# An attention-and-mixer kernel on one core: the second pair's k by SyncE's queue, U and V rounded later, and the first batch's mixing with two channel blocks side by side

## The chip, the cores and the metric

One core of one Trainium2 chip runs the whole program. The time is the device time of one execution in microseconds; the median over several runs counts. Smaller is better.

## The reference, cut to what matters

```python
# q, k, v: (B, H, S, D) = (8, 8, 576, 64);  beacon_k, beacon_v: (8, 8, 16, 64)
k_all = concatenate([beacon_k, k], axis=2)           # 592 keys
v_all = concatenate([beacon_v, v], axis=2)
scores = q @ k_all.T / sqrt(D)                       # causal over the 576, beacons always seen
x = softmax(scores) @ v_all                          # -> (8, 576, 512), heads side by side
h = (x.transpose(0, 2, 1) @ U @ V).transpose(0, 2, 1)   # U: (576, 32), V: (32, 576): mixes tokens
u = x + h
out = u + maximum(u @ w_ch1, 0) @ w_ch2              # w_ch1: (512, 2048), w_ch2: (2048, 512)
```

## The kernel before, in words

Heads are worked in pairs: `p` counts 32 of them, four to a batch, and pair `p` of a batch has the two heads of "set" `c`, which together fill 128 partitions. For a pair, q and k are turned on TensorE (`qkT_units`), the transposed scores are formed and exponentiated on ScalarE (`score_units`, `visit`), and `av_unit` weights v by them and divides by the sums, into `xb`, the batch's attention output with tokens on partitions in five blocks. A batch's four pairs done, the mixing adds `h` and leaves `u` transposed in `uT` (channels on partitions, in four blocks of 128, all 4608 tokens in the free dimension). The MLP then runs over nine blocks of 512 tokens (`mlp_units`: `gps`, L536, and `cps`, L562).

Everything is issued in an order written out by hand. Each engine works through its own queue in that order; only waits on other engines and on transfers hold it up. The change lies in the first 26 us, where the first batch is worked through while loads come in.

**Loads.** Float32 inputs come in two ways. `load_first` has SyncE's and ScalarE's queues bring set 0 of q and k as float32 into `stq` and `stk` (L205); `regroup` (L270) rounds them to float16 into `pr`. `build_masks` has SyncE bring set 1 of q the same way; a memset of one element of the target by VectorE (L126) holds this load back until VectorE gets there. All other loads of q, k, v and the weights are issued by GpSimd (L205, L220, L191), which rounds them on the way into `st`, `vs` and `w`; these are one after the other in GpSimd's queue, each costing GpSimd the time to issue it. Where a pair's k came through GpSimd, `by_heads` turns it in twelve 64-column matmuls (L283), and where it came through `regroup`, `in_pair` turns it in six (L277).

**U and V.** `small_loads` has SyncE load U in three pieces and V as float32 into one tile, `small` (L169 to L174), behind a memset of one element by VectorE (L167). `cast`, further on, has GpSimd round them into `Usb` and `Vsb` (L178, L179) and SyncE copy `Vsb`'s 32 rows to the three other row blocks of 32 partitions (L183), and V's last 80 columns to four places of `Vend` (L184). `Vend[:, cc, :]` is zero except in row block `cc`. So a matmul over all four row blocks, with `Vend[:, cc, :]` as the moving side, picks out channel block `cc`. In the order, `cast` stands on GpSimd right behind the first quarter of `w_ch1` (`emit_w1(0)`, L191) and ahead of the loads of k and q of batch 1.

**The first batch's mixing.** `first_mix` does it in two halves of two channel blocks each:

- `head(c0, n)`: five matmuls `qtp` (L491), one for each block of tokens, with U as the stationary side (32 columns) and 256 channels of `xb` moving; VectorE rounds the result, 32 x 256, into `qts`, named `qfirst` (L494).
- `begin`: matmuls with the identity turn `xb` into PSUM, 496 tokens into `ups` and the last 80 into `uend` (L415).
- `rest`: for each channel block one matmul adds `h` to `ups` and one to `uend`, from `Vsb`'s first 32 rows (L508); ScalarE or VectorE copies them to `uT`.

The first half stands between the two weightings of pair 2 and those of pair 3, the second behind pair 3's, with the first MLP products (`part`, the first token block's `gps`) in between. The later batches (`mix_units`) work with all four channel blocks at once, in four column blocks and then four row blocks (L436, L461) and with `Vend` (L474).

Of the kernel before, what the change touches and what calls it, by code (L numbers as in the profile page):

```python
# [11 lines left out]
F32 = mybir.dt.float32  # L12
# [6 lines left out]
P = 128  # L19
# [11 lines left out]
def kernel(  # L31
# [13 lines left out]
    nc = tc.nc  # L45
    B, H, S, D = q.shape
    Nb = beacon_k.shape[2]
    DM = H * D
    R = moe_U.shape[1]
# [12 lines left out]
    nq = [min(S, P * (j + 1) - Nb) - q0[j] for j in range(NC)]  # L62
    NT = NC
    QM, NL = q0[NT - 1], nq[NT - 1]
    TJ = 6
    TP = S // TJ
    TB = TP + Nb
# [27 lines left out]
    gtp = ctx.enter_context(tc.tile_pool(name="gtp", bufs=2))  # L95
# [9 lines left out]
    def pst(shape, dtype, name):  # L105

        b = emptied.pop(0)
        t = psum.tile(shape, dtype, tag=f"bank{b}", name=name)
        bank_of[id(t)] = (b, t)
        return t  # L110

    def emptying(t):
        emptied.append(bank_of.pop(id(t))[0])
# [8 lines left out]
    def build_masks():  # L122
        make_identity(nc, ident)
        nc.vector.memset(bigmask[:, 0, P - Nb : P], F16_MAX)
        nc.vector.tensor_copy(out=identb, in_=ident)
        nc.vector.memset(first[1][0:1, 2, 0:1], 0.0)  # L126
        token_load(nc.sync, q[0], first[1], SETS[1])
        make_upper_triangular(nc, mask, val=F16_MAX, diag=True)
        token_load(nc.gpsimd, k[0], Ls[0][0][0], SETS[1])
        nc.vector.tensor_copy(out=bigmask[:, 0, 0 : P - Nb], in_=mask[:, Nb:P])  # L130
        nc.vector.tensor_copy(out=bigmask[:, 1, :], in_=mask)
        for i in range(2):
            nc.vector.tensor_scalar(
                out=negmask[:, i, :], in0=bigmask[:, i, :], scalar1=1.0, scalar2=NEG,
                op0=ALU.is_lt, op1=ALU.mult,
            )
        prs[0] = [None, regroup(first, 0, 1, V, act_copy)]
# [10 lines left out]
    Usb = const.tile([P, NT, R], F16, name="Usb", tag="Usb")  # L148

    Vsb = const.tile([P, S], F16, name="Vsb", tag="Vsb")  # L150
    Vend = const.tile([P, NCC, nq[NT - 1]], F16, name="Vend", tag="Vend")
# [12 lines left out]
    def small_loads():  # L164

        f = utp.tile([P, NT * R + S], F32, name="small", tag="ut")
        nc.vector.memset(f[0:1, 0:1], 0.0)  # L167
        uf, vf = f[:, 0 : NT * R].rearrange("p (j r) -> p j r", r=R), f[0:R, NT * R :]
        nc.sync.dma_start(out=uf[: nq[0], 0, :], in_=moe_U[0 : nq[0], :])  # L169
        nc.sync.dma_start(  # L170
            out=uf[:, 1 : NT - 1, :], in_=moe_U[q0[1] : QM, :].rearrange("(j p) r -> p j r", p=P)
        )
        nc.sync.dma_start(out=uf[:NL, NT - 1, :], in_=moe_U[QM:S, :])
        nc.sync.dma_start(out=vf, in_=moe_V)  # L174

        def cast():
            for rr, jj in ((nq[0], slice(0, 1)), (P, slice(1, NT - 1)), (NL, slice(NT - 1, NT))):
                nc.gpsimd.tensor_copy(out=Usb[:rr, jj, :], in_=uf[:rr, jj, :])  # L178
            nc.gpsimd.tensor_copy(out=Vsb[0:R, :], in_=vf)  # L179
            for cc in range(NCC):  # L180
                rs = ds(R * cc, R)
                if cc:
                    nc.sync.dma_start(out=Vsb[rs, :], in_=Vsb[0:R, :])  # L183
                nc.sync.dma_start(out=Vend[rs, cc, :], in_=Vsb[0:R, QM:S])  # L184

        return cast
# [14 lines left out]
    def beacon_load(eng, src, dst, hs):  # L201
        eng.dma_start(out=dst[0:Nb], in_=src[hs].rearrange("h p d -> p h d"))  # L202

    def token_load(eng, src, dst, hs):
        eng.dma_start(out=dst[0:TP, hs, :], in_=src[hs].rearrange("h (p j) d -> p h (j d)", j=TJ))  # L205

    def key_beacons(eng, src, dst, hs):
        beacon_load(eng, src, dst[TP:TB, hs, (TJ - 1) * D : TJ * D], hs)
# [19 lines left out]
    def by_token(t):  # L228
        return t.rearrange("p h (j d) -> p j h d", j=TJ)
# [3 lines left out]
    def qk_tiles():  # L233

        t = [stage.tile([P, TJ * DM], F16, name=f"st{i}", tag=f"st{i}") for i in range(2)]
        st = [x[:, :].rearrange("p (h e) -> p h e", h=H) for x in t]
        whole = [x[:, 0 : NT * DM].rearrange("p (j h d) -> p j h d", h=H, d=D) for x in t]
        return st, whole
# [24 lines left out]
    def regroup(st, c, i, *copies, beacons=True):  # L263

        t = pairs.tile([P, TJ, 2, D], F16, name=f"pr{i}", tag=f"pr{i}")
        src = by_token(st[i][:, 2 * c : 2 * c + 2, :])
        w = TJ // len(copies)
        for a, copy in enumerate(copies):
            js = slice(w * a, w * (a + 1))
            copy(out=t[0:TP, js], in_=src[0:TP, js])  # L270
        if i == 0 and beacons:
            copies[0](out=t[TP:TB, TJ - 1], in_=src[TP:TB, TJ - 1])
        return t
# [139 lines left out]
    def x_into(xb, ups, cc, js, a, first):  # L413
        for j in js:
            nc.tensor.matmul(  # L415
                ups[:, ds(q0[j] - a, nq[j])], xb[: nq[j], j, ts(cc, P)], ident[: nq[j], : nq[j]],
                start=first and j == js[0], stop=False, skip_group_check=True,
            )
# [64 lines left out]
    def first_mix(xb):  # L483

        qts = outp.tile([P, DM], F16, name="qfirst", tag="ob")
        cell = {}

        def head(c0, n):
            qtp = pst([R, P * n], F32, name="qtp")
            for j in range(NT):  # L490
                nc.tensor.matmul(  # L491
                    qtp, Usb[: nq[j], j, :], xb[: nq[j], j, ds(P * c0, P * n)], start=(j == 0), stop=(j == NT - 1)
                )
            nc.vector.tensor_copy(out=qts[0:R, ds(P * c0, P * n)], in_=qtp)  # L494
            emptying(qtp)

        def begin(c0, cs, n=2):
            for cc in cs:
                cell[cc] = pst([P, QM], F32, name="ups")
                x_into(xb, cell[cc], cc, list(range(NT - 1)), 0, True)  # L500
                if cc == c0:
                    cell["end"] = pst([P, n, NL], F32, name="uend")
                x_into(xb, cell["end"][:, cc - c0, :], cc, [NT - 1], QM, cc == c0)

        def rest(c0, n, copies, end):
            for at in (0, QM):
                for i in range(n):
                    nc.tensor.matmul(  # L508
                        cell["end"][:, i, :] if at else cell[c0 + i], qts[0:R, ts(c0 + i, P)],
                        Vsb[0:R, at : S if at else QM], start=False, stop=True, skip_group_check=True,  # L510
                    )
            for cc, copy in zip(range(c0, c0 + n), copies):
                copy(out=uT[:, cc, 0:QM], in_=cell[cc])
                emptying(cell[cc])
            end(out=uT[:, ds(c0, n), QM:S], in_=cell["end"])
            emptying(cell["end"])

        return head, begin, rest
# [114 lines left out]
    Ls, qTs, xbs = {}, {}, {}  # L633
# [35 lines left out]
    SETS = [slice(2 * c, 2 * c + 2) for c in range(NH2)]  # L669

    first = []

    def load_first():

        kf = gtp.tile([P, 2, TJ * D], F32, name="stk", tag="gT")
        qf = gtp.tile([P, 4, TJ * D], F32, name="stq", tag="gT")
        first.extend([kf, qf])
        for src, dst in ((q[0], qf), (k[0], kf)):
            for eng, h in ((nc.sync, 0), (nc.scalar, 1)):
                token_load(eng, src, dst, slice(h, h + 1))  # L680
        Ls[0] = qk_tiles()
        key_beacons(nc.gpsimd, beacon_k[0], Ls[0][0][0], ALLH)
        nc.scalar.activation(out=warm, in_=ones, func=AF.Exp)
# [4 lines left out]
    prs = {}  # L688
    V = nc.vector.tensor_copy
# [122 lines left out]
    with tc.manual_schedule(engines={ENG.PE, ENG.Activation, ENG.DVE, ENG.SP, ENG.Pool}):  # L812
# [12 lines left out]
        idle(IDLE[4], ident)  # L825
        t0[1]()
        sc[0](IDLE[1], gs=[1, 0])
        prs[1] = [None, regroup(first, 1, 1, V)]
        for u in qkT_of(1):
            u()  # L830
        clear()
        cast = small_loads()
        sc[1]([3, 2], False)
        sc = scores_of(1)
# [1 line left out]

        v_tokens(v[0], vss[0], HALVES[1])
        emit_w1(0)
        cast()
        Ls[1] = qk_tiles()  # L840
        (kt, qt), _ = Ls[1]
        token_load(nc.gpsimd, k[1], kt, HALVES[0])
        token_load(nc.gpsimd, q[1], qt, HALVES[0])
        key_beacons(nc.gpsimd, beacon_k[1], kt, ALLH)
        emit_w1(1)
        token_load(nc.gpsimd, k[1], kt, HALVES[1])
# [26 lines left out]
        head, begin, rest = first_mix(xbs[0])  # L873
# [9 lines left out]
        rest(0, 2, (act_copy, act_copy), act_copy)  # L883
        av = av_of(3)
        av[0]()
        av[1]()
        begin(2, (2,))
        part(D0, 2)
        part(D1, 2)
        head(2, 2)  # L890
# [180 lines left out]
    with tc.If(n_bad != 0, label="general"):  # L1071
        with tc.For_i(0, B, 1) as bi:
            L = qk_tiles()
            qT = qkt.tile([P, NH2, S], F16, name="qT", tag="qT")
            xb = xbp.tile([P, NT, DM], F16, name="xb", tag="xb")
# [11 lines left out]
            for t0 in range(0, S, 512):  # L1087
                n = min(512, S - t0)
# [32 lines left out]
```

## Time and profile before

| | us |
|---|---|
| Median of 3 runs (lowest to highest) | 350.36 (350.11 to 350.96) |
| The profiled execution | 349.7 |
| Its span | 348.0 |
| TensorE busy | 341.3 (98%) |
| VectorE busy | 189.7 (55%) |
| ScalarE busy | 163.6 (47%) |
| GpSimd busy | 97.8 (28%) |

The span is what the profiler sees of the program; the execution's time has 1.7 us around it. Engines are called PE (TensorE's matmuls), PEld (its weight loads), DVE (VectorE), ACT (ScalarE), POOL (GpSimd) and SP (SyncE); a `q` behind a name is that engine's issue of transfers. `L491` is line 491 of the kernel before. In the changed kernel the same statement stands a few lines further down. In the timeline a row is start, length, engine, line, operation, out<-in and count, and in brackets the idle time before it with what ended it. `out<-in` are the names in the program, and `x5` is a group of five instructions, merged.

### The profile page before, as it was taken

The page shows a single profiled execution, that of the slowest core. Times are in us where ns is not written, and L with a number is a line of the kernel's source. Part 1 is how long each engine was busy: PE and PEld are TensorE (multiplying, and loading weights), DVE is VectorE, ACT ScalarE, POOL GpSimd, SP SyncE. Part 2 cuts the span into 40 slices and gives each one's busy share as a digit, 9 for nine tenths or more (in the row PEclk, how much of TensorE's full clock was granted, in tenths as well). Part 3 has the DMA queues.
Part 4 walks back from the last instruction along what each step waited for, and adds up shares of the span by engine and source line. Part 5 has one row for each costly group of instructions (what it writes and reads, how often), then busy time and mean ns, then how long its engine had stood idle before and what let it go on. Part 6 is the DMA issues. An engine that isn't in the chain of part 4 may idle for free.

```text
span 348.0 us, 7791 instructions
## 1 busy us (share of the span) xinstructions
PE 341.3 (98%) x3084; PEld 173.2 (50%) x3084; DVE 189.7 (55%) x493; ACT 163.6 (47%) x358; POOL 97.8 (28%) x137
## 2 busy tenths in 40 slices
PE   8899999999999999999999999999999999999995
PEld 4565565455554455444554445455445444444443
DVE  6676965788875553554465556535655542323311
ACT  6957851578723664167615752494434203202300
POOL 8966714544506457303930130000000000000000
PEclk9999999999999999999999999999999999999999
DMA  9999999999999999991999697713122314013011
GB/s 166 135 186 170 169 200 171 216 148 154 128 142 145 167 133 132 154 213 14 146 139 237 64 117 123 184 38 68 62 75 47 69 62 121 2 60 106 17 66 64
DMA packets 146635, 41.88 MB, mean 120 GB/s; under 512 B 131488, under 2 KB 142080, under 8 KB 146592
## 3 DMA queue, kind: packets, MB, share of 16 engines
q0 software_dynamic: 87440, 18.18, 68.2%
q1 hardware_dynamic: 58928, 22.84, 36.0%
q8 instruction: 26, 0.43, 0.5%
q10 hardware_dynamic: 224, 0.30, 0.2%
q14 instruction: 17, 0.14, 0.1%
HBM read 37.37 MB, written 9.44 MB: 134 GB/s over the span
## 4 chain that ended last, share of the span: by engine, by line
PE 93%; POOL 2%; DMA 2%; issue 1%; DVE 1%; ACT 1%; POOLq 0%
PE gps L536 36%; PE cps L562 35%; PE po L399 8%; PE sps L384 6%; DMA st<-in_q_dram 2%; PE tps L277 1%; PE sps L350 1%; POOL vs L220 1%; PE cph L588 1%; PE qtp L436 1%; POOL st L205 1%; PE tps L283 1%; PE ups L461 1%; PE ups L415 1%; ACT expt L356 0%
## 5 line engine op out<-in xcount | busy, mean ns | idle before, releaser
L536 PE MATMUL gps<-uT,w 128*128 128x512 f16 x576 | 136.0, 379 | 0.1
L562 PE MATMUL cps<-w,gT 128*128 128x512 f16 x560 | 130.9, 379 | 0.0
L390 ACT ACTIVATE expt<-sps 128x496 f16<-128x496 f32 x192 | 82.5, 534 | 71.5 <-PE sps L384 71.5
L549 ACT ACTIVATE gT<-gps 128x512 f16<-128x512 f32 x86 | 50.9, 622 | 78.8 <-PE gps L536 78.6
L536 PEld LDWEIGHTS <-w 128*128 128x128 f16 x576 | 51.8, 98 | 58.0 <-issue 2.4
L562 PEld LDWEIGHTS <-gT 128*128 128x128 f16 x560 | 50.8, 98 | 58.9 <-issue 6.2
L551 DVE TENSOR_SCALAR gT<-gps 128x512 f16<-128x512 f32 x58 | 40.0, 690 | 41.9 <-PE gps L536 40.5
L575 DVE TENSOR_TENSOR ob<-cps,ut 128x512 f32<-128x512 f32 x31 | 21.4, 691 | 48.3 <-PE cps L562 47.5
L220 POOL DMA_DIRECT2D vs<-in_v_dram x50 | 39.6, 810 | 17.1 <-PE gps L536 5.8
L399 PEld LDWEIGHTS <-expt 128*128 128x128 f16 (+1 forms) x960 | 36.2, 98 | 12.7 <-issue 0.8
L399 PE MATMUL po<-vs,expt 128*128 128x65 f16 (+1 forms) x960 | 38.9, 194 | 0.0
L408 DVE TENSOR_TENSOR xb<-po,rec 128x320 f16<-128x320 f32 x64 | 31.5, 492 | 2.2
L326 DVE TENSOR_TENSOR expt<-expt,bigmask 128x512 f16<-128x512 f16 x58 | 24.1, 416 | 6.7 <-ACT expt L390 6.7
L356 ACT ACTIVATE expt<-sps 128x496 f16<-128x496 f32 (+2 forms) x64 | 27.1, 584 | 0.9 <-PE sps L350 0.8
L407 DVE RECIPROCAL rec<-po 128x5 f32<-128x5 f32 x64 | 12.1, 188 | 27.0 <-PE po L399 26.8
L384 PE MATMUL sps<-qT,kT 64*128 64x80 f16 (+4 forms) x288 | 23.3, 281 | 0.1
L202 POOL DMA_DIRECT2D vs<-in_beacon_v_dram x8 | 4.3, 536 | 57.8 <-PE po L399 57.7
L384 PEld LDWEIGHTS <-kT 64*128 64x128 f16 x288 | 9.9, 94 | 18.3 <-issue 14.8
L651 POOL DMA_DIRECT2D st<-in_q_dram x20 | 16.9, 863 | 6.6 <-DMA vs<-in_v_dram 2.7
L651 POOL DMA_DIRECT2D st<-in_k_dram x20 | 17.0, 883 | 3.4 <-DMA st<-in_q_dram 3.4
L448 DVE TENSOR_TENSOR uT<-ups,uT 128x496 f16<-128x496 f32 x24 | 14.5, 667 | 5.0 <-PE ups L461 5.0
L310 DVE COPY qT<-tps 128x576 f16<-128x576 f16 (+1 forms) x16 | 11.8, 736 | 4.6 <-PE tps L283 2.8
(98 smaller groups left out, 161.9 us busy)
## 6 DMA issues: line engine op xcount, KB each, us to landing
out_dram<-ob SPq DMA_DIRECT2D x35, 256.0 KB, 2.3
vs<-in_v_dram POOLq DMA_DIRECT2D x18, 128.0 KB, 6.9
w<-in_moe_w_ch_dram POOLq DMA_DIRECT2D x4, 512.0 KB, 6.1
w<-in_moe_w_ch_dram POOLq DMA_DIRECT2D x2, 1024.0 KB, 13.6
st<-in_k_dram POOLq DMA_DIRECT2D x12, 128.0 KB, 8.6
st<-in_q_dram POOLq DMA_DIRECT2D x12, 128.0 KB, 9.6
st<-in_k_dram POOLq DMA_DIRECT2D x2, 576.0 KB, 13.2
st<-in_q_dram POOLq DMA_DIRECT2D x2, 576.0 KB, 16.1
```

Source lines behind the costliest of these rows:

```text
L220: nc.gpsimd.dma_start(out=dst[a : a + nq[j], j, :, :], in_=src[hs, ds(q0[j], nq[j]), :].rearrange("h p d -> p h d"))
L326: nc.vector.tensor_tensor(out=e4, in0=e4, in1=bigmask, op=ALU.min)
L356: nc.scalar.activation(out=ex[i][:, ds(SLOT * g, gw[g])], in_=ps[g, i][:, 0 : gw[g]], func=AF.Exp, scale=scale)
L384: nc.tensor.matmul(ps[p, g, i][:, ds(o, w)], kT[hp, c, ds(P * ch, P)], qT[hp, c, ds(qa, w)], start=True, stop=True,)
L390: nc.scalar.activation(out=at[p][3][i][:, ds(SLOT * g, gw[g])], in_=ps[p, g, i][:, 0 : gw[g]], func=AF.Exp, scale=scale)
L399: nc.tensor.matmul(po[:, j, :], ex[0 : nk[c], ds(blk[(c, j)], P)], vs[0 : nk[c], ds(c * H * E + h * E, E)], start=(c == 0), stop=(c == j),)
L408: nc.vector.tensor_tensor(out=xb[:, :, ds(h * D, D)], in0=po[:, :, 0:D], in1=r.broadcast_to([P, NT, D]), op=ALU.mult)
L536: nc.tensor.matmul(g[:, 0:n], w1[:, cc, ts(dc, P)], uT[:, cc, ds(t0, n)], start=(cc == 0), stop=(cc == NCC - 1))
L549: nc.scalar.activation(out=gT["t"][:, dc, 0:n], in_=g[:, 0:n], func=AF.Relu)
L551: nc.vector.tensor_scalar_max(out=gT["t"][:, dc, 0:n], in0=g[:, 0:n], scalar1=0.0)
L562: nc.tensor.matmul(ps[:m, :], gT["t"][:, dc, ds(P * i, m)], w2[:, dc, :], start=(dc == 0), stop=turned and dc == NDC - 1, skip_group_check ...
L651: nc.gpsimd.dma_start(out=dst[a : m[j], j, :, :], in_=src[:, ds(q0[j], nq[j]), :].rearrange("h p d -> p h d"))
```

## The change

The set 1 of k (pair 1's) is no longer loaded by GpSimd but by SyncE as float32, behind q's, and rounded on VectorE by `regroup`; its 16 beacon rows are copied by VectorE from where GpSimd loads them. V is loaded twice, into two row blocks of `small`, and GpSimd rounds both at once, so that `Vsb` has two row blocks without a copy. `cast` stands two issues later on GpSimd, behind the loads of k and q of the first half of batch 1's heads. In the first mixing, `head` writes its two channel blocks to two column blocks (64 partitions, 128 columns), and `rest` uses one row block for each channel block, and for the last 80 tokens `Vend` with both row blocks. In the second half `begin(2, (2,))` stands ahead of `av[1]`.

```diff
@@ build_masks
-        nc.vector.memset(first[1][0:1, 2, 0:1], 0.0)
-        token_load(nc.sync, q[0], first[1], SETS[1])
+        for x in first[::-1]:
+            nc.vector.memset(x[0:1, 2, 0:1], 0.0)
+        for x, src in zip(first[::-1], (q[0], k[0])):
+            token_load(nc.sync, src, x, SETS[1])
         make_upper_triangular(nc, mask, val=F16_MAX, diag=True)
-        token_load(nc.gpsimd, k[0], Ls[0][0][0], SETS[1])
@@ small_loads
-        uf, vf = f[:, 0 : NT * R].rearrange("p (j r) -> p j r", r=R), f[0:R, NT * R :]
+        uf, vf = f[:, 0 : NT * R].rearrange("p (j r) -> p j r", r=R), f[0 : 2 * R, NT * R :]
...
-        nc.sync.dma_start(out=vf, in_=moe_V)
+        for i in range(2):
+            nc.sync.dma_start(out=vf[ds(R * i, R), :], in_=moe_V)
 
         def cast():
             for rr, jj in ((nq[0], slice(0, 1)), (P, slice(1, NT - 1)), (NL, slice(NT - 1, NT))):
                 nc.gpsimd.tensor_copy(out=Usb[:rr, jj, :], in_=uf[:rr, jj, :])
-            nc.gpsimd.tensor_copy(out=Vsb[0:R, :], in_=vf)
+            nc.gpsimd.tensor_copy(out=Vsb[0 : 2 * R, :], in_=vf)
             for cc in range(NCC):
                 rs = ds(R * cc, R)
-                if cc:
+                if cc > 1:
                     nc.sync.dma_start(out=Vsb[rs, :], in_=Vsb[0:R, :])
                 nc.sync.dma_start(out=Vend[rs, cc, :], in_=Vsb[0:R, QM:S])
@@ first_mix
         def head(c0, n):
-            qtp = pst([R, P * n], F32, name="qtp")
+            qtp = pst([R * n, P], F32, name="qtp")
             for j in range(NT):
-                nc.tensor.matmul(
-                    qtp, Usb[: nq[j], j, :], xb[: nq[j], j, ds(P * c0, P * n)], start=(j == 0), stop=(j == NT - 1)
-                )
-            nc.vector.tensor_copy(out=qts[0:R, ds(P * c0, P * n)], in_=qtp)
+                for i in range(n):
+                    nc.tensor.matmul(
+                        qtp[ds(R * i, R), :], Usb[: nq[j], j, :], xb[: nq[j], j, ts(c0 + i, P)],
+                        start=(j == 0), stop=(j == NT - 1), skip_group_check=True, tile_position=(0, R * i),
+                    )
+            nc.vector.tensor_copy(out=qts[0 : R * n, ts(c0, P)], in_=qtp)
...
         def rest(c0, n, copies, end):
-            for at in (0, QM):
-                for i in range(n):
-                    nc.tensor.matmul(
-                        cell["end"][:, i, :] if at else cell[c0 + i], qts[0:R, ts(c0 + i, P)],
-                        Vsb[0:R, at : S if at else QM], start=False, stop=True, skip_group_check=True,
-                    )
+            for i in range(n):
+                nc.tensor.matmul(
+                    cell[c0 + i], qts[ds(R * i, R), ts(c0, P)], Vsb[ds(R * i, R), 0:QM],
+                    start=False, stop=True, skip_group_check=True,
+                )
+            for i in range(n):
+                nc.tensor.matmul(
+                    cell["end"][:, i, :], qts[0 : R * n, ts(c0, P)], Vend[0 : R * n, i, :],
+                    start=False, stop=True, skip_group_check=True,
+                )
@@ load_first
-        kf = gtp.tile([P, 2, TJ * D], F32, name="stk", tag="gT")
+        kf = gtp.tile([P, 4, TJ * D], F32, name="stk", tag="gT")
@@ the order
-        prs[1] = [None, regroup(first, 1, 1, V)]
+        prs[1] = [regroup(first, 1, i, V, beacons=False) for i in (1, 0)][::-1]
+        V(out=prs[1][0][TP:TB, TJ - 1], in_=by_token(Ls[0][0][0][:, SETS[1], :])[TP:TB, TJ - 1])
...
         emit_w1(0)
-        cast()
         Ls[1] = qk_tiles()
         (kt, qt), _ = Ls[1]
         token_load(nc.gpsimd, k[1], kt, HALVES[0])
         token_load(nc.gpsimd, q[1], qt, HALVES[0])
+        cast()
         key_beacons(nc.gpsimd, beacon_k[1], kt, ALLH)
...
         av = av_of(3)
         av[0]()
+        begin(2, (2,))
         av[1]()
-        begin(2, (2,))
```

## The prediction

> **What bounds the kernel now.** I read the head of the page first, then the chain that ended last in order of time, then the timeline around the edits, and last the landing times of single transfers.
>
> ```profile
> span 348.0 us, 7791 instructions
> PE 341.3 (98%) x3084; PEld 173.2 (50%) x3084; DVE 189.7 (55%) x493; ACT 163.6 (47%) x358; POOL 97.8 (28%) x137
> 9.22 0.60 POOL st L205
> 9.82 5.47 DMA st<-in_q_dram
> 15.34 0.47 PE tps L283 x12
> 16.64 0.58 PE sps L350 x4
> 18.75 0.65 PE qtp L491 x5
> 20.49 0.52 PE ups L508 x2
> 21.01 0.07 PE uend L508 x2
> 23.23 0.65 PE qtp L491 x5
> 24.68 0.52 PE ups L508 x2
> 16.64:20.85 4.21, 4.21 (x75) 2.97 (x75) 3.90 (x15) 3.59 (x10) 4.21 (x7) 1.00 1.17 173
> 20.85:25.20 4.35, 4.35 (x58) 2.65 (x56) 2.27 (x8) 1.41 (x4) 1.52 (x3) 1.00 1.26 196
> 25.20:36.00 10.80, 10.80 (x151) 5.81 (x149) 7.54 (x15) 8.58 (x20) 7.82 (x11) 1.00 1.60 170
> 48.00:348.00 300.00, 295.91 (x2457) 146.84 (x2453) 155.58 (x382) 126.20 (x273) 63.49 (x80) 1.00 1.01 113
> ```
>
> The first two rows are the page's: TensorE is busy for 341.3 of 348.0 us. The next rows are the chain: start, length, what. Up to 9.82 us it runs through GpSimd's issues, then through one q load that lands at 15.29, and from 16.64 on through TensorE. The last four rows are the busy time of each engine in four stretches (after the stretch and its length: PE, PEld, DVE, ACT, POOL, granted clock, DMA share, GB/s). TensorE has no gap in the first three and 4.1 us of gaps in the last 300. So what the change does to TensorE's queue between 16 and 36 us goes to the end one for one: nothing behind it has room to take a delay up, and work removed there is a gain. Ahead of 16.64 the bounds are loads and ScalarE.
>
> **The second mixing, where the saving counts.** In `head`, five matmuls with 256 moving columns become ten with 128 in two column blocks; in `rest`, the two `ups` matmuls get a row block each. The later batches already work so, with four blocks:
>
> ```profile
> 49.23 0.55 PE qtp L436 x20
> 51.64 0.32 PE ups L461 x4
> 54.80 0.14 PE uend L474 x4
> ```
>
> Twenty narrow `qtp` matmuls take 0.55 us on the chain, so ten take 0.28 where five wide ones took 0.65: 0.37 saved if two blocks run side by side as four do, and nothing if they run one after the other (the same number of columns in all). Four `ups` in four row blocks take 0.32; two in one block took 0.52. Two side by side I put at the length of one, 0.26: 0.26 saved, at most 0.36, at least nothing. The two `uend` matmuls stay at 0.07. I take 0.63 us for each mixing (0 to 0.73). VectorE's copy of `qtp` shrinks too, behind other matmuls, so I count nothing. Moving `begin(2, (2,))` ahead of `av[1]` only reorders work that TensorE does anyway: nothing.
>
> **The first mixing, where a wait is added.** Before, the first `uend` matmuls read `Vsb`, which GpSimd itself writes. Now they read `Vend`, blocks 0 and 1, which two transfers on SyncE's queue copy out of `Vsb` after GpSimd's cast. In before nobody needs `Vend` until 54.80 us (the last row above). Behind the waiting matmul in TensorE's queue stand the two weightings of pair 3, the second mixing and the first MLP products: all the rest of the program. So the question is when those two transfers land. Issue times first:
>
> ```profile
> 9.35 0.06 DVE L167 MEMSET small<- 1x1 f32 x1
> 10.80 0.42 SPq L174 DMA_DIRECT2D small<-in_moe_V_dram  x1
> 14.01 0.82 POOL L191 DMA_DIRECT2D w<-in_moe_w_ch_dram  x1
> 14.74 0.49 POOL L178 CAST Usb<-small 112x32 f16<-112x32 f32 x2
> 15.84 0.66 POOL L179 CAST Vsb<-small 32x576 f16<-32x576 f32 x1
> 16.45 0.68 POOL L205 DMA_DIRECT2D st<-in_k_dram  x1
> 16.52 0.65 SPq L184 DMA_DIRECT2D Vend<-Vsb  x1
> 17.12 0.68 POOL L205 DMA_DIRECT2D st<-in_q_dram  x1
> 17.84 0.59 SPq L184 DMA_DIRECT2D Vend<-Vsb  x1
> 20.85 0.23 PE L508 MATMUL uend<-Vsb,qfirst 32*128 32x80 f16 x2
> ```
>
> GpSimd loses one issue early (some 0.63 us, as the 0.60 at 9.22 shows), and its casts move behind the two 0.68 us issues: by its own queue the casts would start at 14.74 - 0.63 + 1.36 = 15.5. But the cast of V also waits for its load, which in before it started right behind: V issued at 10.80, cast at 15.84. That load is issued after VectorE's memset of `small`, and ahead of this memset VectorE now rounds k of pair 1 (0.55, the same shape as the row at 6.25 below) and its beacons (L272 below: 0.19 to 0.52), and may wait for the load. That is 0.75 to 1.1 us later; the second copy of V adds an issue of 0.42. So the second V is issued at about 12.1, and with before's 5.0 us (below) lands at 17.1; the cast (same columns, 0.66) ends at about 17.8, 17.1 if V lands sooner. The first `Vend` copy is issued then, the second 0.65 later, at about 18.1 (17.7 to 18.5).
>
> Now the landings, each the answer on transfers for the stretch of one issue (the last number: us from issue to landing; for the first three rows, medians over issues in the first 30 us):
>
> ```profile
> Vend<-Vsb SPq DMA_DIRECT2D x4, 5.0 KB, 6.0
> small<-in_moe_V_dram SPq DMA_DIRECT2D x1, 72.0 KB, 5.0
> small<-in_moe_U_dram SPq DMA_DIRECT2D x1, 14.0 KB, 2.3
> Vend<-Vsb SPq DMA_DIRECT2D x1, 5.0 KB, 4.5
> Vsb<-Vsb SPq DMA_DIRECT2D x1, 36.0 KB, 7.7
> Vend<-Vsb SPq DMA_DIRECT2D x1, 5.0 KB, 7.2
> w<-in_moe_w_ch_dram POOLq DMA_DIRECT2D x1, 512.0 KB, 6.2
> st<-in_k_dram POOLq DMA_DIRECT2D x1, 288.0 KB, 5.8
> st<-in_q_dram POOLq DMA_DIRECT2D x1, 288.0 KB, 8.1
> ```
>
> A 5 KB copy took 4.5 us when issued at 16.52 and 7.2 when issued at 17.84: it landed at 21.0, then 25.0. The large loads around it landed at 20.2 (weights, 14.01 + 6.2), 22.3 (k) and 25.2 (q). Landings thus follow the order of issue closely: the first copy came in behind the weights, the next two with the q load issued beside them. In the changed kernel both large k and q issues stand ahead of both copies. So I expect the copies at the time of that q load, 24 to 25; the median of 6.0 gives the same, 18.1 + 6.0 = 24.1, and I take that.
>
> [...]
>
> TensorE would be at `uend` at 20.85 - 0.63 = 20.2. It waits 3.9 us. The first mixing's saving and everything earlier disappears in this wait.
>
> **The front, hidden by that wait.** Pair 1's k now takes 0.55 + 0.19 to 0.52 us more on VectorE, ahead of the copies of qT and kT:
>
> ```profile
> 6.25 0.54 DVE L270 CAST pr<-stq 96x768 f16<-96x768 f32 x1
> 8.81 0.16 DVE L315 COPY kT<-tps 128x16 f16<-128x16 f16 x1
> L272 DVE COPY pr<-st x3: 192/397/520, 35.8 to 59.0; 16x128 f16<-16x128 f16 x3
> 9.19 0.58 PE L350 MATMUL sps<-qT,kT 64*128 64x496 f16 x4
> 10.08 0.67 ACT L356 ACTIVATE expt<-sps 128x496 f16<-128x496 f32 x1
> 17.05 3.39 ACT L356 ACTIVATE expt<-sps 128x496 f16<-128x496 f32 x8 [0.23 <-PE sps L350]
> ```
>
> kT of pair 1 was ready at 8.97; it will be at 9.7 to 10.2. Pair 1's scores started 0.22 after it, at 9.19, and four took 0.58; the first is there some 0.4 to 0.6 us after kT, so at 10.1 to 10.8. ScalarE took it at 10.08: a wait of 0 to 0.7 us, against a gain of at most 0.23 (its idle time at 17.05) from q loads issued 0.63 earlier. Net -0.23 to +0.7 at `uend`, and all of it is covered while the copies land after 21; without that cover it counts.
>
> **The sum.** 24.1 - 20.85 = 3.25 later at `uend`, less 0.63 in the second mixing: +2.6 us. On the profiled execution's 349.7 (span 348.0) that is 352.3. That execution lies 0.66 under the median of the runs, 350.36; on the median it gives **353.0 us**.
>
> **The rivals.**
> - *Landing as the first copy did.* No `Vsb` copy stands ahead of the second `Vend` copy any more, so both may land as the first did: 18.1 + 4.5 = 22.6, or 21.6 with the earlier issue. 22.6 - 20.85 - 0.63 = +1.1: 351.5 (350.5 to 351.5). For it: before's first copy was first on its queue too. Against: it was issued when the large q load was not. 17%.
> - *A longer landing,* 7.2 to 7.7 us, since more is ahead: 18.1 + 7.2 = 25.3 to 25.8, or +3.8 to +4.3: 354.2 to 354.7. 13%.
> [...]
> - *The blocks do not run side by side* (the change doesn't do what it says): no saving in the second mixing, wait as forecast: +3.25, 353.6. Against: the rows at 49.23 and 51.64. 5%.
>
> **How the numbers follow.** The forecast has 55%, with 352.0 to 354.2 for landings of 23.1 to 25.3. No change means within 0.3%, 1.05 us: what a measurement can tell here. Of the first rival, 10 points fall within it and 7 above; the no-wait case is faster; all others are slower. Faster 0.10, same 0.10, slower 0.80. The range 350.5 to 354.6 leaves out the no-wait case and the last end of the long landing.
>
> **What would show it.** Right: a wait of TensorE at the `uend` matmul of the first mixing, released by a `Vend` transfer, of 3 to 5 us, with `Vend` landing at 23 to 25 us; TensorE back to back behind it; ten `qtp` in about 0.3 us and two `ups` in about 0.26. Wrong: `Vend` landing before 21 us, or TensorE's gaps after 36 us shrinking by as much as the wait.

## The result, and the profile after

The changed kernel took 355.28 us (median of 6 runs, 354.83 to 357.31) against 350.66 us of the kernel before, measured beside it: a ratio of 1.0133, 95% interval 1.0101 to 1.0165. It is slower by 4.6 us. Forecast were 353.0 us and at most 354.6, so the direction was right and the size was not. The profiled execution took 354.83 us, its span 353.2 us.

The page's head, its row of granted clock in 40 slices, and the chain that ended last in order of time (start, length, what); one row of before, from the same view, stands apart behind them:

```profile
span 353.2 us, 7803 instructions
PE 342.6 (97%) x3088; PEld 173.7 (49%) x3088; DVE 190.3 (54%) x496; ACT 164.2 (47%) x358; POOL 97.4 (28%) x136
PEclk9899999999999999999999999999999999999999
...
3.32 5.90 DMA stk<-in_k_dram
...
14.02 4.18 DMA small<-in_moe_V_dram
...
18.32 0.67 POOL Vsb L181
19.00 0.65 SPq L186
...
19.70 5.82 DMA Vend<-Vsb
...
25.56 0.19 PE uend L516
...
27.90 0.40 PE qtp L494 x10
...
29.10 0.31 PE ups L511 x2
29.41 0.17 PE uend L516 x2
29.59 0.64 PE tps L285 x24
```

```profile
25.27 0.64 PE tps L283 x24
```

TensorE's busy time is 1.3 us longer than before (342.6 us against 341.3) and the span 5.2 us, so most of the difference is standing still. The chain from 14.0 to 25.5 us no longer runs through TensorE but through the load of V, GpSimd's rounding of it, SyncE's issue, and the landing of the second `Vend` copy at 25.5. From there to the transposes at 29.59 TensorE goes back to back. They begin 4.32 us later than in before, and most of the difference in span, 5.2 us, is there already. Of the remaining 0.9 us, 0.4 are lost by the end of the last matmul (348.7 against 344.0) and 0.5 lie behind it; no run looked for their cause. The wait itself, in the view of who waited for whom, is shorter than forecast:

```profile
PE uend L516 <- DMA Vend<-Vsb: 2.2, 2, 1.7
```

It is 2.2 us, not 3.9, since TensorE reached `uend` only at 23.1, 2.3 us later than before and 2.9 later than I had it. The busy time of TensorE in single microseconds shows where, and how it fared in the wait for `Vend` (after the stretch and its length: busy time, instructions, granted clock, DMA share, GB/s):

```profile
7.00:8.00 1.00, 0.77 (x7) 1.00 1.37 195
8.00:9.00 1.00, 0.32 (x6) 1.00 2.26 157
9.00:10.00 1.00, 0.26 (x7) 1.00 2.04 136
10.00:11.00 1.00, 1.00 (x18) 0.79 0.38 24
11.00:12.00 1.00, 1.00 (x11) 0.50 0.81 64
12.00:13.00 1.00, 1.00 (x7) 0.50 1.21 175
13.00:14.00 1.00, 1.00 (x17) 0.50 1.37 127
...
23.00:24.00 1.00, 0.21 (x2) 1.00 1.19 157
24.00:25.00 1.00, 0.08 (x1) 1.00 1.29 200
25.00:26.00 1.00, 0.56 (x13) 1.00 1.28 222
```

TensorE waited for pair 1's q and k, which landed after 5.1 and 5.9 us, and then the granted clock was 0.50 for 3.4 us. In the wait for `Vend`, and behind it, the clock stayed at 1.00. The late front also made `Vend` late, as VectorE's and SyncE's rows of the timeline show:

```profile
8.07 0.56 DVE L272 CAST pr<-stq 96x768 f16<-96x768 f32 x1 [1.39 <-DMA stq<-in_q_dram]
...
9.24 0.56 DVE L272 CAST pr<-stk 96x768 f16<-96x768 f32 x1 [0.62 <-DMA stk<-in_k_dram]
...
12.08 0.06 DVE L168 MEMSET small<- 1x1 f32 x1
...
13.55 0.89 SPq L176 DMA_DIRECT2D small<-in_moe_V_dram  x2
...
19.00 1.27 SPq L186 DMA_DIRECT2D Vend<-Vsb  x2
```

VectorE waited for q and then for k of pair 1. So its memset of `small` came at 12.08 instead of 9.35, V's second load was issued at 14.0 (the prediction had 12.1), and the second `Vend` copy at 19.70 (the prediction had 18.1). The late front is one candidate cause. The wait for `Vend` is the other. The experiments take them apart.

### The profile page after: what moved, and what is told of

Read it like the earlier page. It is cut to its first block, busy times and chain, and to the rows that moved or that the text cites. A ratio compares the mean times of both kernels' runs of the same rounds, so it can differ in the third digit from the quotient of the medians.

```text
span 353.2 us, 7803 instructions
## 1 busy us (share of the span) xinstructions
PE 342.6 (97%) x3088; PEld 173.7 (49%) x3088; DVE 190.3 (54%) x496; ACT 164.2 (47%) x358; POOL 97.4 (28%) x136
## 4 chain that ended last, share of the span: by engine, by line
PE 89%; DMA 5%; DVE 2%; issue 1%; SPq 1%; ACT 1%; POOL 0%; POOLq 0%
PE gps L544 35%; PE cps L570 35%; PE po L401 7%; PE sps L386 6%; DMA stk<-in_k_dram 2%; DMA Vend<-Vsb 2%; DMA small<-in_moe_V_dram 1%; PE tps L279 1%; PE cph L596 1%; PE qtp L438 1%; PE sps L352 1%; PE ups L463 1%; PE tps L285 1%; ACT expt L358 0%; PE ups L417 0%
## 5 line engine op out<-in xcount | busy, mean ns | idle before, releaser
L409 DVE RECIPROCAL rec<-po 128x5 f32<-128x5 f32 x64 | 12.1, 189 | 29.1 <-PE po L401 28.9
```

## The experiments

Times are medians, and ratios are to the kernel before run beside each group (350.94 us for experiments 1 to 4, 350.62 for 5 to 8, 350.60 for 9 and 10).

**1. k back on GpSimd, all else as changed.**

```diff
-        for x, src in zip(first[::-1], (q[0], k[0])):
-            token_load(nc.sync, src, x, SETS[1])
+        token_load(nc.sync, q[0], first[1], SETS[1])
...
+        token_load(nc.gpsimd, k[0], Ls[0][0][0], SETS[1])
...
-        prs[1] = [regroup(first, 1, i, V, beacons=False) for i in (1, 0)][::-1]
-        V(out=prs[1][0][TP:TB, TJ - 1], in_=by_token(Ls[0][0][0][:, SETS[1], :])[TP:TB, TJ - 1])
+        prs[1] = [None, regroup(first, 1, 1, V)]
```

> The changed kernel with pair 1's k loaded by GpSimd again; all else as changed. Theory A (two costs: k's load on SyncE's queue makes TensorE come late to the first uend, 23.1 us instead of about 20.4, and the Vend copies, issued later for the same reason, make it wait there until 25.6): the front is back where it was, V's second load lands at about 16.3, GpSimd's cast ends at about 17.3, the second Vend copy is issued at 18.0 and lands some 5.9 us later, at 23.9; TensorE waits about 3.3 us there; the time is about 353.5. Rival B (k's load costs nothing, since the wait for Vend covers it; Vend comes late by the casts' new place): uend still starts at about 25.5 and the time stays near 355.2. Rival C (Vend's wait was only the consequence of the late front): Vend lands before 21.5, time under 351.

Measured: 355.19 us, ratio 1.0109 (1.0063 to 1.0155). Nothing was regained. The chain of waits, the waits of TensorE, and TensorE by single microseconds:

```profile
18.65 5.73 DMA Vend<-Vsb
...
24.41 0.22 PE uend L515
...
26.88 1.71 PE gps L543 x4
...
30.61 0.64 PE tps L284 x24
```

```profile
PE uend L515 <- DMA Vend<-Vsb: 3.2, 2, 2.9
```

```profile
21.00:22.00 1.00, 0.00 (x0) 1.00 1.34 210
22.00:23.00 1.00, 0.00 (x0) 0.79 1.19 146
23.00:24.00 1.00, 0.15 (x1) 0.50 1.24 202
24.00:25.00 1.00, 0.66 (x11) 0.50 1.25 215
...
28.00:29.00 1.00, 1.00 (x12) 0.50 1.72 175
29.00:30.00 1.00, 1.00 (x13) 0.80 2.33 151
```

The front is as early as in before, `Vend` lands at 24.4 (forecast for the change: 24.1), and TensorE waits 3.2 us. What neither theory had: 1.6 us into the wait, at 22.6, TensorE's granted clock falls to 0.50 and stays there until 29.4. Four `gps` matmuls take 1.71 us on the chain, where they took 0.86 to 0.87 in other traces here (below). So here the wait has a second price, paid after it. The regained front and this price go against each other: the time is that of the changed kernel, whose profiled execution paid the first and not the second.

**2. `Vend`'s two blocks written by GpSimd; k still by SyncE.**

```diff
                 if cc > 1:
                     nc.sync.dma_start(out=Vsb[rs, :], in_=Vsb[0:R, :])
-                nc.sync.dma_start(out=Vend[rs, cc, :], in_=Vsb[0:R, QM:S])
+                if cc > 1:
+                    nc.sync.dma_start(out=Vend[rs, cc, :], in_=Vsb[0:R, QM:S])
+                else:
+                    nc.gpsimd.tensor_copy(out=Vend[rs, cc, :], in_=vf[rs, QM:S])
```

> The changed kernel, but the two blocks of Vend that the first mixing reads are written by GpSimd from the loaded V (two small roundings of 32x80 behind the cast of V), not by transfers. k is still loaded by SyncE. Theory A: TensorE does not wait at uend, which starts at about 23.1 instead of 25.6 (second one): 2.4 us of the 4.6 go, about 352.9. Rival B (the late front costs nothing of its own): uend at about 20.5, about 350. Rival C: no change, 355.2, as the wait only moves to another landing.

Measured: 351.58 us (349.83 to 354.06), ratio 1.0023 (0.9994 to 1.0053). The median lies between the 352.9 of theory A and the 350 of rival B. TensorE no longer waits for `Vend`, and in the profiled execution its clock stays at 1.00. Without the transfer most of the loss is gone: the wait for `Vend` carries it.

**3. Both of these edits together.**

> The changed kernel with both of these edits: k by GpSimd and Vend's two blocks by GpSimd. What is left of the change is the side-by-side mixing, V loaded twice, and the casts behind two issues. Theory A: no wait at uend, TensorE there at about 20.4; the two mixings each save what the changed kernel's trace shows, 0.25 in qtp and 0.21 in ups, less 0.10 in uend, 0.36 each: 349.9 against 350.66 before. Rival: the casts, ending at 17.7, or the two 5 KB roundings are too late for the ups matmuls, and the time is at or above before's 350.7.

Measured: 350.37 us, ratio 0.9974 (0.995 to 0.9998). The side-by-side mixing without its transfer is a small gain, as theory A had it (expected 349.9 at a before of 350.66, so 0.7 us; measured 0.57 us between the medians, 0.9 by the ratio, and the interval ends just short of 1). Not all that TensorE saves reaches the end. In the profiled execution (351.13 us) the transposes begin 0.56 us earlier than in before, and then TensorE stands still for 0.8 us at 59.9 and for 0.6 at 63.0, waiting for VectorE's work on later pairs. Experiment 2 differs from this one in k's load alone, and its median is 1.2 us higher. So k by SyncE may cost that much where no wait covers it; experiment 4 puts it at 0.3 us.

**4. k's part alone, on the kernel before.** The edit is the changed kernel's, as in the diff above.

> The kernel before with k's part of the change alone (set 1 of k by SyncE as float32, rounded on VectorE). Theory A: q of pair 1 lands at about 8.05 instead of 6.25, k at 9.2, and GpSimd waits about 1 us before its third k load; TensorE reaches the first mixing about 2.5 us later, and this goes through to the end: about 353.1. Rival B: the delay is caught up before the mixing, within 0.5 us of before: 350.7 to 351.2.

Measured: 351.29 us, ratio 1.0007 (0.9981 to 1.0033), nine of the ten runs from 350.51 to 352.92, one at 356.83. Rival B (350.7 to 351.2) holds for the median, theory A's 353.1 does not. The chain:

```profile
3.33 4.57 DMA stk<-in_k_dram
...
20.92 0.52 PE ups L509 x2
```

In this execution k landed after 4.6 us, not 5.9, and TensorE reached the mixing 0.43 us later than before (20.49), as the prediction had bounded it. In experiment 2's profile, with the same load, k took 4.5 us. So the 5.9 us and the low clock in the front of the changed kernel's profile are not what this load always brings. Why it takes 4.5 us in one execution and 5.9 in another stays open.

**5. The wait filled: 13 matmuls into an unused bank ahead of the `uend` that waits, on the kernel of experiment 1.**

```diff
-        def rest(c0, n, copies, end):
+        def rest(c0, n, copies, end, warm=0):
...
+            if warm:
+                idle(warm, ident)
             for i in range(n):
                 nc.tensor.matmul(
                     cell["end"][:, i, :], qts[0 : R * n, ts(c0, P)], Vend[0 : R * n, i, :],
...
-        rest(0, 2, (act_copy, act_copy), act_copy)
+        rest(0, 2, (act_copy, act_copy), act_copy, 13)
```

> The kernel of e1 (k by GpSimd, Vend's blocks by transfer), with 13 matmuls of 128x512 into an unused bank put between the first ups and the first uend matmuls: TensorE works for about 2.8 us where it would wait. They add nothing to the result. Theory A (the wait costs twice: its own 3.2 us, and then 6.8 us at a granted clock of 0.5, because TensorE stood idle): the clock stays at 1.0, the second uend still starts at about 24.4, the next products run at full rate, and the time falls from 355.2 to about 351.9 to 353.5 (1.7 to 3.3 us less). Rival D (the clock falls for another reason, such as the load of transfers): the clock falls all the same and the time stays at 355 or rises.

Measured: 353.39 us, ratio 1.007 (1.0042 to 1.0097); the mean granted clock was 0.997 to 1.0 in each of the ten runs. The chain and the waits:

```profile
24.24 0.35 PE uend L517 x2
...
25.88 0.86 PE gps L545 x4
...
28.42 0.64 PE tps L284 x24
```

```profile
PE uend L517 <- DMA Vend<-Vsb: 0.3, 1, 0.3
```

The two `uend` are done at the same time as in experiment 1 (24.6), with useless work in place of the wait. Yet the transposes start at 28.42, not 30.61, and the time falls by 1.8 us between the medians, 1.4 by the ratios. That is the price of the fallen clock. What is left over before, 2.8 us (2.5 by the ratio), is the wait itself, and close to the +2.6 that the prediction had for the whole change.

**6. The casts back at their old place, on the kernel of experiment 1** (`cast()` behind `emit_w1(0)`).

> The kernel of e1 with the casts back at their old place, ahead of the k and q loads of batch 1. Theory A with landings in the order of issue: the second V still lands at about 17.1, so the cast still ends at about 17.9 and the copies are issued at 17.9 and 18.6, but the k and q loads are no longer ahead of them; they land some 4.5 us after issue, at about 22.5 to 23, and the wait shrinks by 1.5 us: about 352 to 353.5. Rival E (landings do not depend on what stands ahead; SyncE's copies take 5.6 to 5.9 us here anyway): uend at 24.4, time 355, and k and q of batch 1, issued 2 us later, may add a second wait.

Measured: 355.21 us, ratio 1.0117 (1.0062 to 1.0172). The tile's view, its landing times, and TensorE's wait:

```profile
DMA to landing us min/median/max: 3.8/5.5/5.7
```

```profile
PE uend L515 <- DMA Vend<-Vsb: 2.7, 2, 2.2
```

GpSimd was held until V's second load (16.6), and so the large loads were issued beside the copies and not behind them:

```profile
17.92 0.68 POOL L206 DMA_DIRECT2D st<-in_q_dram  x1
```

The second copy was issued at 18.02, 0.1 us behind this q load. The first copy landed after 3.8 us, the second after 5.6. So the wait became only 0.5 us shorter, the clock fell again (0.50 from 23.65 to 27.07), and the time did not move. The expected gain was not there. This did not yet separate the two theories of the landing; experiment 10 does.

**7. Experiment 3 with the casts at their old place.**

> The kernel of e3 (k by GpSimd, Vend's two blocks by GpSimd) with the casts at their old place. Theory A: no wait at the mixing in either place, so 350.4 as e3, unless GpSimd, now waiting for the second V until about 17.2 ahead of the k and q loads of batch 1, issues these some 2 us late and TensorE waits for the q load at its next transposes (25 us): then up to 2 us more, 350.4 to 352.4.

Measured: 351.91 us, ratio 1.0025 (0.9998 to 1.0052), where experiment 3 had 0.9974. The wait that was named in advance is there, a load of batch 1 that GpSimd issued late:

```profile
PE tps L287 <- DMA st<-in_beacon_k_dram: 0.6, 1, 0.6
```

Experiment 8, measured beside it with the casts at the later place, took 350.37. So with V loaded twice the later place of the casts is worth about 1.5 us; no run has it with V loaded once.

**8. Experiment 3 with `begin(2, (2,))` back behind both weightings of pair 3.**

> The kernel of e3 with the third channel block's transposes back behind both weightings of pair 3. Theory A: the same work in another order, the same time, 350.4 (within 0.3). Rival: the order hides VectorE's division behind those transposes, and undoing it costs up to 0.4 us.

Measured: 350.37 us, ratio 0.9982 (0.9956 to 1.0007), the same as experiment 3 within the intervals. The order makes no difference that these runs can tell.

**9. Six matmuls in place of 13.**

> The kernel of e1 with 6 instead of 13 matmuls of 128x512 into an unused bank ahead of the uend that waits: TensorE works for about 1.3 us and then waits for about 2 us. They add nothing to the result. Theory A (what brings the clock down is the length of the gap, seen in stretches of 3.4 us; a gap of 2.2 us in the changed kernel's profile left it up, 2.7 us in e6 took it down): the clock stays at 1.0 in most executions, 353.4 as with 13. Rival D: any wait of this kind brings it down, 355.

Measured: 354.23 us, ratio 1.0103 (1.007 to 1.0137). In the profiled execution the gap was 1.7 us and the clock stayed up:

```profile
PE uend L517 <- DMA Vend<-Vsb: 1.7, 1, 1.7
```

But the four runs fall into two kinds: 352.97 and 353.54 us with a mean clock of 0.998 to 0.999, and 354.91 and 354.92 us with 0.995. So the clock probably fell in two of them. Only the run of 353.54 us has a trace, so how long TensorE stood still in the others is not known. The expectation (353.4, the clock up in most executions) is right for half of the runs.

**10. Batch 1's k and q loads held until `Vend` has landed** (on the kernel of experiment 6).

```diff
         emit_w1(0)
         cast()
+        for i in range(2):
+            nc.gpsimd.tensor_copy(out=warm[0 : 2 * R, :], in_=Vend[0 : 2 * R, i, 0:1])
```

> The kernel of e6 (k by GpSimd, casts ahead of batch 1's loads), with two one-column reads of Vend by GpSimd ahead of the k and q loads of batch 1, so that these are issued only when Vend's two blocks have landed. The time itself is not the point: those loads come late and TensorE will wait for them. Theory A (a small copy lands behind what was issued ahead of it on the same 16 DMA engines): with only the first quarter of w_ch1 ahead, both copies land 3 to 4 us after issue, at about 21 to 21.5, not 5.6. Rival E (the copies take 5.6 us whatever is ahead or beside): landing at 23.6 as in e6.

The landing was the question. In the chain and in the tile's view:

```profile
18.97 3.02 DMA Vend<-Vsb
```

```profile
DMA to landing us min/median/max: 1.7/3.1/3.4
```

With the large loads out of the way the two copies landed after 3.2 and 3.0 us. Beside those loads they had taken 5.3 to 6.1, but for the 3.8 of experiment 6's first. Theory A holds here: with batch 1's loads held, the copies of 5 KB took 2.1 to 3.1 us less (0.6 to 0.8 less than that 3.8). In two traces the second copy lands close to batch 1's q load, which was issued ahead of it: copy and load at 25.5 and 25.5 in the changed kernel, 23.6 and 24.1 in experiment 6. With that load held it landed at 22.0. The order is not strict: in the changed kernel the second quarter of `w_ch1`, whose issue had begun 0.25 us ahead of the copy's, landed 2.8 us behind it. The kernel took 355.24 us in its one run, as those loads now came late.

## Why the prediction was right or wrong

- *TensorE bounds the span, and what happens to its queue goes to the end:* right for the delay, only in part for a saving. The transposes were 4.32 us late and the span 5.2 us longer. But in experiment 3 TensorE, 0.56 us ahead of before at the transposes, stood waiting for VectorE later on.
- *The new wait is for `Vend`, blocks 0 and 1, and lasts until a landing at about 24.1:* right in the mechanism, and in the landing as experiment 1 has it, 24.4. The latency of the second copy was taken as 6.0 and measured 5.7 there and 5.8 in the changed kernel. In the changed kernel's profile this copy was issued at 19.70, not 18.1, as the front was late there.
- *Landings follow the order of issue:* right as far as these runs go, though not strictly (experiment 10). A 5 KB copy took 5.3 to 6.1 us beside GpSimd's loads (3.8 once) and 3.0 to 3.2 with batch 1's held back.
- *A step that failed: "It waits 3.9 us" was the whole price of the wait.* I priced a standing TensorE by the length of its wait alone. In experiment 1 the granted clock was 0.50 for 6.8 us, in a wait of 3.2 us and behind it, and experiment 5 prices that at 1.4 to 1.8 us. For experiment 1's kernel, the prediction's 353.0 plus that is 354.4 to 354.8; measured were 355.19.
- *A step that failed: the front is "hidden by that wait".* The front did not stay behind the wait, it moved the wait's end. The prediction let VectorE's memset of `small` come 0.75 to 1.1 us later, and put the wait for pair 1's loads, which it names ("may wait for the load"), at nothing. In the profiled execution of the change VectorE stood 1.4 and 0.6 us for these loads, the memset came 2.7 us later, and `Vend` landed at 25.5, 1.4 us later than forecast. TensorE came 2.3 us late, not 0.7 at most, so that it waited less, and its clock did not fall there. For this execution, 352.3 were forecast and 354.83 measured. The 2.5 us between are this landing (1.4), the smaller saving in the second mixing (0.3) and the time lost behind the transposes (0.9).
- *Luck:* the miss came about in two ways, and that both give nearly the same number is luck. With the front early, the copies land at 24.4 and the clock falls (experiment 1, 355.19); with the front late, they land at 25.5 and the clock stays up behind the wait (the changed kernel's profile). Which of the two the other five runs of the changed kernel had is open. All six had a mean granted clock of 0.987 to 0.994, while the twelve of experiment 3 had 0.997 to 1.0.
- *0.63 us saved in a mixing:* too much. Ten `qtp` took 0.40 (0.28 forecast), two `ups` 0.31 (0.26), and the two `uend`, now from 64 rows, 0.17 instead of 0.07. That is 0.36 us for each mixing. The prediction left `uend` at 0.07. Two blocks are not as good as half of four: the runs do not show why.
- *The rivals:* the no-wait case and the early landing did not occur. The longer landing, +3.8 to +4.3, came nearest the number, but for another reason than the one that it gave. The 10% for a faster kernel rest on the no-wait case, copies that land before TensorE arrives. No run shows such a landing beside GpSimd's loads: in the changed kernel and in experiments 1 and 6 TensorE waited 2.2, 3.2 and 2.7 us for them.

## What to carry to other kernels

Where a transfer moves onto the path of the engine that bounds the span, take its landing time from transfers issued at the same moment of the same stage, with the same loads ahead of it, not from its size: the 5 KB copies took 5.3 to 6.1 us beside GpSimd's loads (3.8 once) and 3.0 to 3.2 with batch 1's held back. Follow the moment of its issue back through every queue that it depends on. Reckon that a new wait of TensorE may cost its length and, behind it, work at half clock: in and behind waits of 3.2 and 2.7 us the granted clock was 0.50 for 6.8 and 3.4 us (experiments 1 and 6), while with one of 2.2 us (the changed kernel) it stayed at 1.00. Filling the wait with idle matmuls took that second price away here, 1.4 to 1.8 us (experiment 5). Better still, let an engine write the small operand in place of the transfer: two roundings of 32 x 80 on GpSimd took 0.2 to 0.4 us each here and brought a loss of 1.3% down to 0.2%, which the runs cannot tell from none; with k back on GpSimd as well it became a gain of about 0.2%, at the edge of what they can tell.

## What the runs showed of the hardware that was not expected

TensorE need not stand still to lose its clock: with busy shares of 0.77, 0.32 and 0.26 in three successive microseconds it was granted 0.50 for the next 3.4 us. Nor does standing still always cost it: with 0.21, 0.08 and 0.56 in the wait for `Vend` it kept 1.00 in the same execution.

The clock changed at 10.58 and 14.00 in the changed kernel, at 22.57 and 29.40 in experiment 1, at 23.65 and 27.07 in experiment 6. So the stretches at 0.50 are 3.42, 6.83 and 3.42 us long: one, two and one step of 3.41 us. In the step just before each of these falls TensorE was idle for 1.66, 1.63 and 2.70 us. In the changed kernel two such steps, counted on from 14.00, hold the wait for `Vend`. They have 1.03 and 1.13 idle us, and the clock stayed up; it also stayed up in experiment 9's profiled execution with its wait of 1.7 us. Whether the clock goes by the idle time in such a step, and by how much of it, was not shown. Where the changes lie differs from execution to execution.
